# An unbroken warm-up, a reordered front and another load order in a fused attention and feed-forward kernel

## The chip, the cores and the metric

The kernel runs on one core of a Trainium2 chip. The metric is device time in microseconds (us) of one execution, lower is better. Most executions of the kernel before agree within 0.3%. A run is called slow when it is over 1.5% above the fastest of the same kernel; comparisons use the other runs ("fast" ones). One run of each kernel was also profiled; all places in time below are from those profiles, counted from the first instruction.

## The reference, cut to what matters

```python
# x (8, 8, 512, 64), state (8, 8, 32, 64); w_in (512, 2048), w_out (2048, 512)
a  = softmax(scale * x @ state^T);   xread = a @ state      # per batch and head
a2 = softmax(scale * state @ x^T);   sread = a2 @ x
y  = concat(xread, sread) over the sequence, heads side by side   # (8 * 544, 512)
h  = y @ w_in;  r = max(h, 0);  g = s * r * r + b;  out = g @ w_out
```

The kernel never forms xread: it multiplies state with a 512-column part of w_in first (M), and then h = a @ M.

## The kernel before

The work is eight batches. A batch needs x with its two inner axes exchanged (xT), the state likewise (stT), the scores T = state @ x^T, E = exp(T), the sums D, the four products M with a cast each, then 16 times h, relu, square, and products with w_out (o). Each step is handed to a small planner with an estimate of its duration. The planner simulates the engines and fixes, before anything runs, the order in which every engine executes its steps. At run time an engine takes its instructions in that order, also when one waits for a load and others behind it are ready: in the profile of the changed kernel, below, VectorE stands 4.08 us before a cast whose load is late, with a copy ready behind it, and TensorE 3.30 us.

The parts that the change and the argument touch (cuts marked):

```python
# 1. The loads. GpSimd issues the large ones in this order; "stf1" is the state of the
#    second and third batches, issued by SyncE behind a memset that GpSimd makes.
SEQ = "wi0 x1 wi1 stf1 wo0 wi2 wo1 wi3 wo2 wo3 x2 sb x3 x4 x5"
...
elif it[0] == "stf1":       # -3.0: the planner expects it 3.0 us before the load ahead of it
    load(key, 0.3, -3.0, late(stf1, st_v[:, NG : NB_HW * NG, :]), [it], after=3.4)

# 2. The casts of the state: one step of VectorE serves the second and third batches
add(DV(0.4), 0, lambda e: cast_st(e, stf1, NG, n1), [("stf1",)], [("st", 1), ("st", 2)])

# 3. The state of the other five: GpSimd makes a 128x2 copy first, only so that the load
#    isn't issued before the last w_out part has landed
def load_stf2(e):
    nc.gpsimd.tensor_copy(stf2[:, 0, 0:2], wo[3][:, 0, 0:2])
    nc.sync.dma_start(stf2, st_v[:, NB_HW * NG :, :])

# 4. xT of the first three batches (NB_HW = 3) is made by TensorE (xT_mm) and copied by
#    VectorE; of the others by four DMA transposes each, issued by SyncE
...
# 5. Warm-up: the planner puts a product of a zero tile wherever TensorE has nothing ready
def filler(e):
    mm(ob[1], warm[:, 0:P], warm)
for step in sorted(plan.order(filler, 14.0, landed), key=lambda t: t[:2]):
    step[3](step[2])
```

The softmax here doesn't subtract the row's maximum and nothing guards it: scores larger than these inputs give would overflow.

Of the kernel before, what the change touches and what calls it, by code (L numbers as in the profile page):

```python
# [13 lines left out]
class Plan:  # L14
# [13 lines left out]
    def order(self, filler, fill_until, ready):  # L28
# [24 lines left out]
        free_at["PE"] = 1.2  # L53
        mode, channel, log, now, done_n = False, 7.0, [], 0.0, 0
        times = []

        def soon(i):
# [14 lines left out]
        while done_n < len(ops):  # L72
            for e in free_at:
# [29 lines left out]
                if best is None:  # L103
                    fill = 0.43 if now < 7.0 else 0.22
                    if e == "PE" and now < fill_until and not any(since[i] < now + fill for i in cand[e]):
                        free_at[e] = now + fill
                        times.append(free_at[e])
                        log.append((now, len(log), "PE", filler, "warm", free_at[e]))
                    continue
# [47 lines left out]
def kernel(  # L157
# [119 lines left out]
    def late_dma(dst, src):  # L277
# [5 lines left out]
    K = dict(  # L283
        h1=4.4, hs=0.6, M0=-5.6, M1=0.9, T1=0.0, x2=24.6, T2=23.7, D2=27.2, M2=35.3, V0=27.7, V1=21.3, u=12.3,
        us=5.1, pd1=12.5, o0=13.1, o2=23.0, w=26.2, r=0.5, T=-9.8, D=3.1, Mb=6.4, V=8.6, S=3.6, S0=0.1, E=-0.5,
        L=-6.2, a4=-4.7, Mc=1.5, pd=13.4, solo=2.0, hsr=-4.1, Ssr=0.0,
    )
# [61 lines left out]
    for i in range(4):  # L349
        add(  # L350
            (DV(0.35), AC(0.5)),
            -29 + i,
            cast_x0(i),
            [("xf", i)],
            [("x", 0, i)],
            [("u", f"xf{i // 2}"), ("xn", "x0")],
        )
# [44 lines left out]
    nc.gpsimd.tensor_copy(gate, ident16[:, 0:2])  # L402
    SEQ = "wi0 x1 wi1 stf1 wo0 wi2 wo1 wi3 wo2 wo3 x2 sb x3 x4 x5"
    seq = [(t,) if t in ("stf1", "sb") else (t[:-1], int(t[-1])) for t in SEQ.split()]
    for n, it in enumerate(seq):
        key = -40 + n
        if it[0] == "wi":
            load(key, 0.8, 4.2 if it[1] == 0 else 2.8, load_wi(it[1]), [it], after=3.4)
        elif it[0] == "wo":
            load(key, 0.8, 2.8, load_wo(it[1]), [it], after=3.4)  # L410
        elif it[0] == "x":
            b = it[1]
            load(
                key, 0.9, 2.9 if b == 1 else 3.9, load_x(b),
                [("x", b, i) for i in range(4)], [("xn", f"x{b}")], after=3.4,
            )
        elif it[0] == "stf1":
            load(key, 0.3, -3.0, late(stf1, st_v[:, NG : NB_HW * NG, :]), [it], after=3.4)
        else:
            load(key, 0.15, 0.1, late(s_bc, moe_s.to_broadcast((P, 1))), [("s",)], after=3.4)  # L420
            load(key + 0.1, 0.15, 0.1, late(b_bc, moe_b.to_broadcast((P, 1))), [("b",)], after=3.4)
# [28 lines left out]
    add(("SP", 1.5), 18, dma_stT, [("st", 3)], [("stT", b) for b in range(NB_HW, B)], land=("tp", 3.0))  # L450

    def xT_of(b, h):
        if b < NB_HW:
            return A[b]["xT"][:, h % 2, h // 2]
        return A[b]["xT"][:, h]

    def dma_xT(b, i):
        def fn(e):
            if "xT" not in A[b]:
                A[b]["xT"] = apool.tile([P, H, 2, P], FP16, name=f"xT_{b}", tag="xT")  # L460
                A[b]["stT"] = stTd[:, (b - NB_HW) * NG : (b - NB_HW + 1) * NG]
            nc.sync.dma_start_transpose(
                A[b]["xT"][:, 2 * i : 2 * i + 2].rearrange("p h k q -> p (h k) q"),
                xn[b][:, 2 * i : 2 * i + 2].rearrange("p h c d -> p (h c d)"),
            )

        return fn
# [34 lines left out]

    def xT_copy(b, i):
        def fn(e):
            if i == 0:
                A[b]["xT"] = apool.tile([P, 2, 4, 2, P], FP16, name=f"xT_{b}", tag="xT")
            copy_on(e, A[b]["xT"][:, i], A[b][f"xTps{i}"])

        return fn

    def st_T(b, g, q, m):
        h = head_of(g, q)
        return A[b]["stT"][64 * m : 64 * m + 64, h // 4, 32 * (h % 4) : 32 * (h % 4) + 32]

# [146 lines left out]

    for b in range(B):
        if b < 2:
            kT = kD = kx = -10 if b == 0 else K["T1"]
            kM = [8 * c + (K["M0"] if b == 0 else K["M1"]) for c in range(4)]
        elif b == 2:
# [8 lines left out]
        if b < NB_HW:  # L675
# [3 lines left out]
            add(DV(0.2), kx, stT_copy(b), [("stps", b)], [("stT", b)], [stps] + stT_b)  # L679
            for i in range(2):  # L680
                ps = ("att", f"xTps{b}{i}")
                xs = [("x", b, 2 * i), ("x", b, 2 * i + 1)]
                add(PEt(0.45), kx + 0.1 * i, xT_mm(b, i), xs, [("xTps", b, i)], [ps, xn_b, xT_b])
                add(
                    (DV(0.62), AC(1.1)) if b == 9 else DV(0.62), kx + 0.1 * i, xT_copy(b, i),
                    [("xTps", b, i)] + ([("xT", b, 0)] if i else []), [("xT", b, i)], [ps, xT_b],
                )
        else:
            stT_b = []
            for i in range(4):  # L690
                add(
                    ("SP", 1.2), kx + 0.1 * i, dma_xT(b, i),
                    [("x", b, i)], [("xT4", b, i)], [xT_b, xn_b], ("tp", 3.0),
                )
        xT_need = [("xT", b, 0), ("xT", b, 1)] if b < NB_HW else [("xT4", b, i) for i in range(4)]
        E_b = [("E0", f"E{b}0"), ("E1", f"E{b}1"), ("rs", f"rs{b}")]
        Tb = [("att", f"T{b}0"), ("att", f"T{b}1")]
        if b == 0:
            for g in range(2):
                add(  # L700
                    PEt(0.2), kT, T_mm(b, [g]), [("stT", b), xT_need[g]] + ([("T", b, 0)] if g else []),
                    [("T", b, g)], Tb + [xT_b] + stT_b + E_b, tiled=True,
# [6 lines left out]
        for g in range(2):  # L709
# [3 lines left out]
            add(  # L713
                AC(0.73), kT + K["E"] + g, E_exp(b, g), [("T", b, g)] + ([("E", b, 0)] if g else []),
                [("E", b, g)], Tb + [Eb, rs],
            )
            add(PEt(0.22), kD, D_mm(b, g), [("E", b, g)], [("D", b, g)], [Eb, Dps, Rb, a4b])
            add(AC(0.53), kD + K["L"] + g, D_ln(b, g), [("D", b, g)], [("Dl", b, g)], [Dps])
            add(AC(0.53), kD + K["L"] + g, D_exp(b, g), [("Dl", b, g)], [("R", b, g)], [Dps, Rb])
            add(DV(0.34), kD + K["a4"], a4_mul(b, g), [("R", b, g)], [("a4", b, g)], [Eb, Rb, a4b])  # L720
# [10 lines left out]
        for c in range(4):  # L731
# [5 lines left out]
            for g in range(2):  # L737
                kc = kM[c] + K["Mc"]
                add(
                    (AC(0.53), DV(0.6)) if g else (DV(0.6), AC(0.53)), kc, M_cast(b, c, g),  # L740
                    [("Mps", b, c)], [("M", b, c, g)], [mp[g], M_b],
                )
# [77 lines left out]
    for b in range(B):  # L820
        for f in range(NKF):
# [7 lines left out]
            )  # L829
            add((AC(0.5), DV(0.6)) if b < 2 else AC(0.5), k + K["r"], relu(b, f, S), [("h", b, f)], [("r", b, f)], [hb, gb])  # L830
            add(DV(0.335), k, square(b, f), [("r", b, f)], [("g", b, f)], [gb])
# [256 lines left out]
    def filler(e):  # L1088
        mm(ob[1], warm[:, 0:P], warm)

    landed = {
        "ident": 3.2, "stf": 4.8, ("xf", 0): 3.8, ("xf", 1): 4.7, ("xf", 2): 5.8, ("xf", 3): 6.8,
    }
# [30 lines left out]
```

## Time and profile before

| | before |
|---|---|
| time, median of 4 runs | 216.97 us (216.32 to 216.99) |
| span of the profiled run | 215.0 us |
| TensorE busy | 204.7 us, 95% |
| matrix work of its own at full clock, worked out below | 193.3 us |
| TensorE's last product | 208.4 us |

I took the start of every product from the trace and gave each kind the time that it takes in an unbroken row at full clock: 0.2155 us for 512 columns, 0.0555 for a transpose, 0.0428 for a product of M, 0.0223 for one of T, 0.0109 for one of V. What half and full clock are is read from the profile of before: 512-column products in a row start 0.427 us apart up to 9.94 us and 0.216 apart from 10.97 on, and the trace's record of the granted clock opens at 10.56, with 1.00; later in a profile half clock is a granted clock of 0.50. Elapsed time minus the own work begun so far is the **time lost so far**: fillers, holes and half clock together. A reading at one moment says how far a kernel is behind; the difference between two moments says where it fell behind. Before has lost 13.8 us at 25 us, and 15.1 at the end: all but 1.4 us of the loss lies in the first 25 us.

### The profile page before, as it was taken

To read this page: it belongs to the slowest core of one execution; us is meant where nothing else is said; L and a number is where in the kernel's file an instruction comes from. 1 tells how busy PE (TensorE), PEld (TensorE's weight loads), DVE (VectorE), ACT (ScalarE), POOL (GpSimd) and SP (SyncE) were. 2 spreads that over 40 slices of the span, in tenths; PEclk is the share of its full clock that TensorE was granted. 3 is DMA by queue.
4 is the path that set the end of the run, shared out by engine and by line. 5 is a ranking of instruction groups with operands and counts; after the bars stand their busy time and mean duration, and the time that the engine had idled before them with its cause. 6 is when DMAs were issued, how large, how long until landed. Compare 5 with 4: busy or idle time off the path is not lost.

```text
span 215.0 us, 4963 instructions
## 1 busy us (share of the span) xinstructions
PE 204.7 (95%) x1976; PEld 132.6 (62%) x1976; DVE 176.0 (82%) x412; ACT 132.5 (62%) x288; POOL 37.3 (17%) x60
## 2 busy tenths in 40 slices
PE   5998999999999999999999999999999999999980
PEld 1452334544567676667666766676667777888860
DVE  1258999999998969999999998999999988776750
ACT  4478997695385965795579558855786544532000
POOL 4923100050134261012101210121012102100000
PEclk9999999999999999999999999999999999999997
DMA  6999999999379996453164203311232011210221
GB/s 191 188 196 184 207 204 196 184 153 213 88 128 189 148 200 127 100 102 102 49 100 109 99 30 45 82 52 66 59 81 85 17 48 55 101 36 15 99 83 64
DMA packets 41415, 24.05 MB, mean 112 GB/s; under 512 B 25776, under 2 KB 39600, under 8 KB 41392
## 3 DMA queue, kind: packets, MB, share of 16 engines
q0 software_dynamic: 13840, 15.21, 35.9%
q1 hardware_dynamic: 26992, 8.40, 23.6%
q8 instruction: 15, 0.25, 0.5%
q10 hardware_dynamic: 560, 0.13, 0.3%
q14 instruction: 8, 0.07, 0.1%
HBM read 17.37 MB, written 8.91 MB: 122 GB/s over the span
## 4 chain that ended last, share of the span: by engine, by line
PE 84%; ACT 5%; DVE 5%; DMA 2%; issue 1%; SPq 0%
PE o L209 47%; PE h L209 22%; PE Mps L209 4%; PE h_sr L209 3%; PE osr L209 3%; ACT g L773 2%; DMA xf<-in_x_dram 2%; DVE g L779 1%; PE D L209 1%; ACT M L310 1%; PE V L209 1%; PE xTps L209 1%; PE T L209 1%; ACT E L540 1%; DVE u L858 1%
## 5 line engine op out<-in xcount | busy, mean ns | idle before, releaser
L773 ACT ACTIVATE g<-h 128x512 f16<-128x512 f32 x126 | 73.4, 601 | 41.5 <-PE h L209 41.3
L209 PE MATMUL h<-a,M 128*128 128x512 f16 x256 | 73.8, 380 | 0.6 <-ACT g L773 0.5
L779 DVE TENSOR_TENSOR g<-g 128x512 f16<-128x512 f16 x128 | 52.7, 420 | 3.9 <-ACT g L773 2.3
L209 PEld LDWEIGHTS <-pd 128*128 128x128 f16 x448 | 42.6, 98 | 20.0 <-issue 3.4
L209 PEld LDWEIGHTS <-g 128*128 128x128 f16 x400 | 39.0, 98 | 19.6 <-issue 0.6
L209 PE MATMUL o<-u,pd 128*128 128x256 f16 x336 | 45.9, 273 | 0.0
L209 PE MATMUL o<-wo,g 128*128 128x256 f16 (+1 forms) x288 | 45.5, 297 | 0.1
L1030 POOL DMA_DIRECT2D out_dram<-c x24 | 16.3, 679 | 103.8 <-DVE c L1018 101.0
L209 PEld LDWEIGHTS <-M 128*128 128x128 f16 x256 | 24.1, 98 | 13.2 <-issue 4.6
L310 ACT CAST M<-Mps 128x512 f16<-128x512 f32 x45 | 25.3, 595 | 7.1 <-PE Mps L209 7.1
L1018 DVE SCALAR_TENSOR_TENSOR c<-o,s_bc,bias_bc 128x512 f32<-128x512 f32 x28 | 21.0, 750 | 7.4 <-PE o L209 6.5
L795 DVE TENSOR_TENSOR pd<-g 128x1024 f16<-128x1024 f16 x28 | 19.2, 686 | 0.3
L1018 DVE SCALAR_TENSOR_TENSOR c<-o,s_bc,c 128x512 f32<-128x512 f32 x21 | 15.7, 750 | 1.8 <-PE o L209 1.6
L209 PE MATMUL o<-wo,pd 128*128 128x256 f16 x112 | 16.2, 273 | 0.0
L209 PE MATMUL o<-u,g 128*128 128x256 f16 x112 | 15.5, 273 | 0.0
L312 DVE CAST M<-Mps 128x512 f16<-128x512 f32 x19 | 13.0, 687 | 2.0 <-PE Mps L209 1.9
L773 ACT ACTIVATE g_sr<-h_sr 128x256 f16<-128x256 f32 x16 | 6.1, 383 | 10.5 <-PE h_sr L209 10.4
L540 ACT ACTIVATE E<-T 128x256 f16<-128x256 f32 x32 | 11.8, 389 | 1.1 <-PE T L209 1.1
L806 DVE TENSOR_TENSOR pd<-g,pd 128x512 f16<-128x512 f16 x28 | 11.8, 422 | 0.4
L387 POOL DMA_DIRECT2D xn<-in_x_dram x13 | 10.4, 818 | 8.6 <-DMA wi<-in_moe_w_in_dram 4.0
L804 DVE TENSOR_TENSOR pd<-g,pd 128x512 f16<-128x512 f16 x28 | 11.7, 418 | 0.0
L559 ACT ACTIVATE D<-D 128x512 f32<-128x512 f32 x16 | 9.6, 601 | 2.0 <-PE D L209 1.9
(71 smaller groups left out, 165.1 us busy)
## 6 DMA issues: line engine op xcount, KB each, us to landing
out_dram<-c POOLq DMA_DIRECT2D x24, 256.0 KB, 2.5
xn<-in_x_dram POOLq DMA_DIRECT2D x5, 512.0 KB, 22.4
wi<-in_moe_w_in_dram POOLq DMA_DIRECT2D x4, 512.0 KB, 13.2
wo<-in_moe_w_out_dram POOLq DMA_DIRECT2D x4, 512.0 KB, 18.8
xf<-in_x_dram SPq DMA_DIRECT2D x4, 256.0 KB, 3.4
out_dram<-osb POOLq DMA_DIRECT2D x4, 256.0 KB, 4.1
xn<-in_x_dram POOLq DMA_DIRECT2D x8, 128.0 KB, 4.4
out_dram<-c SPq DMA_DIRECT2D x4, 256.0 KB, 2.5
```

The costliest lines, as they stand in the source:

```text
L209: return nc.tensor.matmul(out, lhsT, rhs, start=start, stop=stop, tile_position=tp, is_transpose=is_transpose, skip_group_check=True,)
L310: nc.scalar.copy(dst, src)
L312: ENG[e].tensor_copy(dst, src)
L387: nc.gpsimd.dma_start(out=xn[b][:, h0:h1].rearrange("p h c d -> p h (c d)"), in_=x[b, h0:h1].rearrange("h (q c) d -> q h (c d)", q=P),)
L540: nc.scalar.activation(a["E"][g][:, 256 * m : 256 * m + 256], a["T"][m][:, g, :], AF.Exp, scale=scale, accum_out=a["rs"][:, g, m : m + 1],)
L773: nc.scalar.activation(g_of(name, f), OSB["h", name, f], AF.Relu)
L779: ENG[e].tensor_mul(g_of(name, f), g_of(name, f), g_of(name, f))
L795: nc.vector.tensor_tensor(pd[:, :, 0:2], g4[:, :, 1:2, :].to_broadcast((P, 2, 2, t)), g4[:, :, 0:4:3, :], ALU.subtract,)
L804: nc.vector.tensor_tensor(pd[:, :, 2], g4[:, :, 3], pd[:, :, 0], ALU.subtract)
L806: nc.vector.tensor_tensor(pd[:, :, 3], g4[:, :, 2], pd[:, :, 2], ALU.subtract)
L1018: nc.vector.scalar_tensor_tensor(t, src, s_bc, add, ALU.mult, ALU.add)
L1030: ENG[e].dma_start(dst[:, rows:SCH:2, hD * h : hD * h + hD], SN[b, name])
```

## The change

The intent: bring the array to full clock sooner (nine fillers in a row), let the second batch's attention start before w_in is there (its x is loaded first), take the third batch's 16 transposes off TensorE, and give the planner more places to set (new keys, ScalarE or VectorE for every relu). Cut to its core:

```diff
+        for k in range(9):                       # planner: nine fillers in one row at 1.2 us
+            log.append((free_at["PE"], len(log), "PE", filler, "warm", free_at["PE"] + 0.43))
+            free_at["PE"] += 0.43
...
-                    fill = 0.43 if now < 7.0 else 0.22
+                    fill = 0.22
...
-    SEQ = "wi0 x1 wi1 stf1 wo0 wi2 wo1 wi3 wo2 wo3 x2 sb x3 x4 x5"
+    SEQ = "x1 wi0 stf1 wo0 wi1 wi2 wi3 wo1 wo2 wo3 sb x2 x3 x4 x5"
...
-            load(key, 0.3, -3.0, late(stf1, st_v[:, NG : NB_HW * NG, :]), [it], after=3.4)
+            load(key, 0.3, -2.2, late(stf1, st_v[:, NG : NB_HW * NG, :]), [it], after=3.4)
...
+    NB_T = 2                                     # xT by TensorE for two batches, not three
-        if b < NB_HW:
+        if b < NB_T:
             return A[b]["xT"][:, h % 2, h // 2]
...                                               # K: most keys changed, some 20 added;
                                                  # half copies of xT for the first batch
```

More of the change, by code (lines that the diff above doesn't have):

```diff
@@ L53, in order @@
         free_at["PE"] = 1.2
-        mode, channel, log, now, done_n = False, 7.0, [], 0.0, 0
+        mode, channel, log, now, done_n = False, 7.2, [], 0.0, 0
         times = []
+        for k in range(9):
+            log.append((free_at["PE"], len(log), "PE", filler, "warm", free_at["PE"] + 0.43))
+            free_at["PE"] += 0.43
         def soon(i):
@@ L283 @@
     K = dict(
-        h1=4.4, hs=0.6, M0=-5.6, M1=0.9, T1=0.0, x2=24.6, T2=23.7, D2=27.2, M2=35.3, V0=27.7, V1=21.3, u=12.3,
-        us=5.1, pd1=12.5, o0=13.1, o2=23.0, w=26.2, r=0.5, T=-9.8, D=3.1, Mb=6.4, V=8.6, S=3.6, S0=0.1, E=-0.5,
-        L=-6.2, a4=-4.7, Mc=1.5, pd=13.4, solo=2.0, hsr=-4.1, Ssr=0.0,
+        h1=4.3, hs=0.6, M0=0.0, M1=0.9, T1=-1.4, x2=24.6, T2=25.1, D2=23.6, M2=34.0, V0=27.7, V1=29.1, u=11.8,
+        us=2.5, pd1=11.8, o0=12.8, o2=20.7, w=24.9, r=0.5, T=-9.7, D=3.1, Mb=6.4, V=0.6, S=3.6, S0=0.4, E=-0.7,
+        L=-4.9, E0=-7.0, L0=-5.0, E1=-7.0, L1=0.5, a4=-7.1, Mc=1.5, pd=13.4, solo=2.0, f0=0.0, f1=8.0, mc=0.3,
+        hsr=-2.4, Ssr=4.1, jE00=0.0, jE01=-1.8, jL00=-1.9, jL01=-0.3, jR00=0.0, jR01=0.0, jE10=2.5, jE11=0.0,
+        jL10=0.0, jL11=0.0, jR10=0.0, jR11=1.8, jM0=0.0, jM1=0.0,
     )
@@ L350 @@
         add(
-            (DV(0.35), AC(0.5)),
+            AC(0.5) if i < 3 else (DV(0.35), AC(0.5)),
             -29 + i,
@@ L407 @@
         if it[0] == "wi":
-            load(key, 0.8, 4.2 if it[1] == 0 else 2.8, load_wi(it[1]), [it], after=3.4)
+            load(key, 0.8, 2.62, load_wi(it[1]), [it], after=3.4)
         elif it[0] == "wo":
-            load(key, 0.8, 2.8, load_wo(it[1]), [it], after=3.4)
+            load(key, 0.8, 2.62, load_wo(it[1]), [it], after=3.4)
         elif it[0] == "x":
@@ L413 @@
             load(
-                key, 0.9, 2.9 if b == 1 else 3.9, load_x(b),
+                key, 0.9, {1: 3.4, 2: 2.9}.get(b, 3.9), load_x(b),
                 [("x", b, i) for i in range(4)], [("xn", f"x{b}")], after=3.4,
@@ L460, in fn @@
                 A[b]["xT"] = apool.tile([P, H, 2, P], FP16, name=f"xT_{b}", tag="xT")
-                A[b]["stT"] = stTd[:, (b - NB_HW) * NG : (b - NB_HW + 1) * NG]
             nc.sync.dma_start_transpose(
@@ L501, in xT_mm, with xT_copy @@
         return fn
-    def xT_copy(b, i):
+    def xT_copy(b, i, q0=0, q1=4):
         def fn(e):
-            if i == 0:
+            if "xT" not in A[b]:
                 A[b]["xT"] = apool.tile([P, 2, 4, 2, P], FP16, name=f"xT_{b}", tag="xT")
-            copy_on(e, A[b]["xT"][:, i], A[b][f"xTps{i}"])
+            copy_on(e, A[b]["xT"][:, i, q0:q1], A[b][f"xTps{i}"][:, q0:q1])
         return fn
@@ L512, in st_T @@
         h = head_of(g, q)
-        return A[b]["stT"][64 * m : 64 * m + 64, h // 4, 32 * (h % 4) : 32 * (h % 4) + 32]
+        t = A[b]["stT"] if b < NB_HW else stTd[:, (b - NB_HW) * NG : (b - NB_HW + 1) * NG]
+        return t[64 * m : 64 * m + 64, h // 4, 32 * (h % 4) : 32 * (h % 4) + 32]
     def T_mm(b, gs):
@@ L662 @@
     for b in range(B):
+        kE, kL = K["E"], K["L"]
         if b < 2:
             kT = kD = kx = -10 if b == 0 else K["T1"]
+            kE, kL = (K["E0"], K["L0"]) if b == 0 else (K["E1"], K["L1"])
             kM = [8 * c + (K["M0"] if b == 0 else K["M1"]) for c in range(4)]
@@ L679 @@
             add(DV(0.2), kx, stT_copy(b), [("stps", b)], [("stT", b)], [stps] + stT_b)
-            for i in range(2):
+            for i in range(2 if b < NB_T else 0):
                 ps = ("att", f"xTps{b}{i}")
@@ L683 @@
                 add(PEt(0.45), kx + 0.1 * i, xT_mm(b, i), xs, [("xTps", b, i)], [ps, xn_b, xT_b])
-                add(
-                    (DV(0.62), AC(1.1)) if b == 9 else DV(0.62), kx + 0.1 * i, xT_copy(b, i),
-                    [("xTps", b, i)] + ([("xT", b, 0)] if i else []), [("xT", b, i)], [ps, xT_b],
-                )
+                if b == 0:
+                    for n in range(2):
+                        add(
+                            DV(0.35) if i == 0 else (DV(0.35), AC(0.56)), -29.5 + 10 * i, xT_copy(b, i, 2 * n, 2 * n + 2),
+                            [("xTps", b, i)] + ([("xTh", b, 0, 0), ("xTh", b, 0, 1)] if i else []),
+                            [("xTh", b, i, n)], [ps, xT_b],
+                        )
+                else:
+                    add(
+                        DV(0.62), kx + 0.1 * i, xT_copy(b, i),
+                        [("xTps", b, i)] + ([("xT", b, 0)] if i else []), [("xT", b, i)], [ps, xT_b],
+                    )
         else:
             stT_b = []
+        if b >= NB_T:
             for i in range(4):
@@ L694 @@
                 )
-        xT_need = [("xT", b, 0), ("xT", b, 1)] if b < NB_HW else [("xT4", b, i) for i in range(4)]
+        xT_need = [("xT", b, 0), ("xT", b, 1)] if b < NB_T else [("xT4", b, i) for i in range(4)]
         E_b = [("E0", f"E{b}0"), ("E1", f"E{b}1"), ("rs", f"rs{b}")]
@@ L700 @@
                 add(
-                    PEt(0.2), kT, T_mm(b, [g]), [("stT", b), xT_need[g]] + ([("T", b, 0)] if g else []),
+                    PEt(0.2), kT, T_mm(b, [g]), [("stT", b), ("xTh", b, g, 0), ("xTh", b, g, 1)] + ([("T", b, 0)] if g else []),
                     [("T", b, g)], Tb + [xT_b] + stT_b + E_b, tiled=True,
@@ L713 @@
             add(
-                AC(0.73), kT + K["E"] + g, E_exp(b, g), [("T", b, g)] + ([("E", b, 0)] if g else []),
+                AC(0.73), kT + kE + g + K.get(f"jE{b}{g}", 0.0), E_exp(b, g), [("T", b, g)] + ([("E", b, 0)] if g else []),
                 [("E", b, g)], Tb + [Eb, rs],
@@ L717 @@
             add(PEt(0.22), kD, D_mm(b, g), [("E", b, g)], [("D", b, g)], [Eb, Dps, Rb, a4b])
-            add(AC(0.53), kD + K["L"] + g, D_ln(b, g), [("D", b, g)], [("Dl", b, g)], [Dps])
-            add(AC(0.53), kD + K["L"] + g, D_exp(b, g), [("Dl", b, g)], [("R", b, g)], [Dps, Rb])
+            add(AC(0.53), kD + kL + g + K.get(f"jL{b}{g}", 0.0), D_ln(b, g), [("D", b, g)], [("Dl", b, g)], [Dps])
+            add(AC(0.53), kD + kL + g + K.get(f"jR{b}{g}", 0.0), D_exp(b, g), [("Dl", b, g)], [("R", b, g)], [Dps, Rb])
             add(DV(0.34), kD + K["a4"], a4_mul(b, g), [("R", b, g)], [("a4", b, g)], [Eb, Rb, a4b])
@@ L737 @@
             for g in range(2):
-                kc = kM[c] + K["Mc"]
+                kc = kM[c] + K["Mc"] + K.get(f"jM{b}", 0.0)
                 add(
                     (AC(0.53), DV(0.6)) if g else (DV(0.6), AC(0.53)), kc, M_cast(b, c, g),
-                    [("Mps", b, c)], [("M", b, c, g)], [mp[g], M_b],
+                    [("Mps", b, c)], [("M", b, c, g)], [mp[g], M_b], spare=K["mc"],
                 )
@@ L829 @@
             )
-            add((AC(0.5), DV(0.6)) if b < 2 else AC(0.5), k + K["r"], relu(b, f, S), [("h", b, f)], [("r", b, f)], [hb, gb])
+            add((AC(0.5), DV(0.6)), k + K["r"], relu(b, f, S), [("h", b, f)], [("r", b, f)], [hb, gb], spare=K["f0"] if b < 2 else K["f1"])
             add(DV(0.335), k, square(b, f), [("r", b, f)], [("g", b, f)], [gb])
@@ L1091 @@
     landed = {
-        "ident": 3.2, "stf": 4.8, ("xf", 0): 3.8, ("xf", 1): 4.7, ("xf", 2): 5.8, ("xf", 3): 6.8,
+        "ident": 3.2, "stf": 4.8, ("xf", 0): 3.9, ("xf", 1): 4.75, ("xf", 2): 6.2, ("xf", 3): 6.4,
     }
```

## The prediction

> **What bounds the kernel now.** I read the page's busy shares first, then the busy table by stretch, then TensorE's instructions in order of time, then the chain of work that ended last, and at the end the landing times of the loads.
>
> ```profile
> PE 204.7 (95%) x1976; PEld 132.6 (62%) x1976; DVE 176.0 (82%) x412; ACT 132.5 (62%) x288; POOL 37.3 (17%) x60
> PE 84%; ACT 5%; DVE 5%; DMA 2%; issue 1%; SPq 0%
> 0.00:10.00 10.00, 7.47 (x38) 3.27 (x38) 2.40 (x8) 4.50 (x9) 6.85 (x14) 1.00 0.89 191
> 20.00:30.00 10.00, 9.53 (x61) 3.43 (x60) 8.94 (x25) 9.72 (x20) 0.94 (x2) 1.00 1.24 203
> 50.00:60.00 10.00, 10.00 (x142) 4.98 (x140) 9.55 (x23) 4.92 (x10) 0.54 (x1) 1.00 0.73 104
> 150.00:170.00 20.00, 20.00 (x216) 13.77 (x201) 18.12 (x42) 14.60 (x32) 2.03 (x3) 1.00 0.26 69
> ```
>
> The columns of the last four lines are the stretch in us, its length, busy us of PE, PEld, DVE, ACT and POOL (instruction counts in brackets), the granted clock, the DMA share and GB/s. From 50 us on TensorE is full, without a hole, until its last instruction. So the kernel is a fixed amount of matrix work plus whatever TensorE does not spend on that work in the first 50 us. A change gains only by taking away matrix work, or by taking away filler and holes in that first part. Everything after 50 us shifts along with it.
>
> The busy share hides the filler: products of a zero tile ("o<-warm") count as busy. TensorE's own list shows them, and what they stand between:
>
> ```profile
> 1.19 2.31 PE L209 MATMUL o<-warm 128*128 128x512 f16 x5 [1.19 <-DVE warm L224]
> 4.64 0.61 PE L209 MATMUL xTps<-ident,xn 128*128 128x128 f16 x4 [1.14 <-ACT xn L310]
> ...
> 8.66 1.06 PE L209 MATMUL o<-warm 128*128 128x512 f16 x2
> 9.51 0.64 PE L209 MATMUL D<-E,bones 128*128 128x512 f16 x1
> ...
> 12.48 0.41 PE L209 MATMUL Mps<-wi,stT 64*32 64x512 f16 x8
> 12.82 1.69 PE L209 MATMUL o<-warm 128*128 128x512 f16 x7
> 14.35 1.03 PE L209 MATMUL h<-a,M 128*128 128x512 f16 x4
> ...
> 17.97 0.90 PE L209 MATMUL Mps<-wi,stT 64*32 64x512 f16 x8
> 19.56 0.74 PE L209 MATMUL D<-E,bones 128*128 128x512 f16 x2 [0.69 <-ACT E L540]
> 20.14 1.09 PE L209 MATMUL h<-a,M 128*128 128x512 f16 x4
> 21.15 0.41 PE L209 MATMUL Mps<-wi,stT 64*32 64x512 f16 x8
> 21.50 1.90 PE L209 MATMUL o<-wo,g 128*128 128x512 f16 x8
> ...
> 38.19 1.06 PE L209 MATMUL xTps<-ident,xn 128*128 128x128 f16 x16
> ```
>
> Lengths overlap in this list, so I use differences of starts. There are 24 fillers before 14.35 us. Of these 14.35 us only about 2.1 are the kernel's own work at full speed; the rest is filler, half speed and waiting. After that the largest hole is the group at 17.97: the next one starts 1.59 us later, where eight such products otherwise take 0.34 (12.48 to 12.82), so 1.25 us are lost. Between 24.75 and 27.34 two groups of four h products take 1.31 and 1.28 us where four take 0.86, some 0.85 us more.
>
> The chain of waits says who holds TensorE there: from 16.84 to 26.06 us it runs over ScalarE alone (relu, casts of M, the exponentials of the second batch), which is busy 9.72 of 10 us.
>
> [...] the fillers at 8.66 start 0.425 apart, the seven at 12.82 take 1.53 us, 0.219 each, and the switch lies at about 10.4 us. The granted clock in the table above stays at 1.00 through this, so it doesn't show it. The 1.14 us hole before 4.64 is the break which the change closes.
>
> [...] The trace shows them landing in the order of issue. By issue time plus time to landing: first w_in part 3.4 + 6.6 = 10.0; second batch's x 4.3 + 9.3 = 13.6; second w_in part 5.2 + 11.1 = 16.3; first w_out part 6.2 + 12.7 = 18.9; third w_in part 6.9 + 15.2 = 22.1. So 2.6 us for each weight part, 3.6 for an x, about 3.2 with the state load between. [...]
>
> [...] Here SyncE issues them, 1.19 to 1.93 us for each xT piece, median 3.6 us to landing, 8.9 for the transposes of a that are issued while loads still run.
>
> **The change part by part.** The order of the changed kernel's instructions is known from building it; its times are not.
>
> 1. Third batch's x is transposed by DMA instead of TensorE. It takes away 16 products, 38.19 to 39.08, 0.89 us of TensorE on the path, and two VectorE copies (1.28 us, off the path, since VectorE leads no wait there). It adds four transposes to SyncE, and moves that batch's scores to well after the first output products of the second batch. Gain 0.89.
>
> 2. The fillers: nine in one row after 1.2 us (eleven before the first real product), 25 in all against 24. I expect the array warm at 5 to 8 us instead of 10.4. That makes the first batch's transposes, T and D shorter (0.83 us for eight transposes at 7.83, 0.44 for eight at 15.21; D 0.43 to 0.22), and the filler in front of a ready instruction too. About 1 us off the chain to the first h. I count it as zero by itself, since part 3 makes that first h wait for a load.
>
> 3. Second batch's x in front, first w_in part behind. By the landings above, x comes at 10.0 + 1.0 = 11.0 and w_in at 13.6, where x came. The M products then start at about 13.8, take 0.34, and the cast (0.6 to 0.69) with two hand-overs of about 0.1 makes the first h start at about 15.0: 0.65 later than 14.35. But in place of fillers the second batch's 16 transposes (0.88), state transpose (0.12), T (0.36) and M (0.34) now stand ahead of it or at it. Then D of both batches and four h follow, and the next M products need the second w_in part, which is fourth in the queue: about 18.9. At 18.9 + 0.2 the M products of both batches run, 0.34 + 0.23, and at 19.67 this much is done: all transposes, T, D and two M of both batches, four h. The old kernel has done that and two h more at 21.50, so it was there at 21.50 - 0.87 = 20.63. Gain 0.96.
>
> 4. The first batch's steps: four half copies of xT (a 1024-column copy takes 0.69, a 256-column one 0.28, so a half about 0.42), one of them on ScalarE, the first three casts of x on ScalarE as they were. T can start some 0.3 us earlier, again hidden behind the load. The choice of engine for relu in later batches is hardly used: VectorE does one relu instead of two and 17 casts of M instead of 19. Zero.
>
> 5. From 20 to 50 us the same ScalarE work has to pass; the holes there (0.45 and 0.42 at 24.75 and 26.06, 0.31 at 33.2) I leave as they are. The old hole at 17.97 is part of the sum in 3.
>
> 6. Cost: later w_out parts. The second moves from 7.65 + 17.0 = 24.7 to 27.2, and the third batch's DMA transposes: stTd is issued at 44.60 and takes 3.01, so three of the four xT pieces come after 47.6, end issuing at 47.6 + 3 x 1.45 = 52.0 and land about 3 later, near 55, just about where T of the third batch stands in the new order; the fourth batch's follow at once. I put half a chance on a hole of 0.2, the rest being absorbed. Cost 0.1.
>
> Sum: 0.89 + 0.96 - 0.1 = 1.75 us off 216.99, or 215.2. Spread over the runs of before is 0.67 us. I round to 215.1, because the earlier full clock may also shorten the way to the first h a little, of which I counted nothing.
>
> **The rivals.**
> A: the warm-up is what counts. Then the first h would come about a microsecond before 14.35, and with the 0.89 and the reordering the time would fall by 2.5 to 3, to about 214.2. For it: TensorE is at half speed for two thirds of the way to the first h. Against it: TensorE's products there are few, and w_in cannot be in before about 13.6.
> B: ScalarE takes all of the gain of the start back, since it is 97% busy from 20 to 30 us and the chain lies on it. Moving the second batch's exponentials forward into ScalarE's holes (1.39 us before its logarithm at 10.19, 0.70 and 0.78 at 14.98 and 16.84) speaks against it. It would leave only 0.89: 216.1.
> C: the DMA transposes of the third batch come late and TensorE stands still at T or the D after it, for 1 to 3 us. For it: the arithmetic of part 6, and 8.9 us to landing while loads run. Against it: the loads are over by 47.6 and the order leaves output products in front of T. It would give 216 to 218.
> D: later w_out parts stop VectorE, which takes its work strictly in order, at the sums over w_out; squares stand behind them. 0.5 us at most: 215.6.
>
> **Range and chances.** The parts that I trust are 0.89 (removed work on a full engine) and about 1 for the start; A adds up to 1, B, C or D take up to 1 or a little more. 8 times in 10: 214.0 to 216.5. Two per cent is 4.3 us, as much as all the holes that I found after 14.35 and the transposes together, so faster by over 2% is 0.03. Slower by over 2% needs C at its worst: 0.02. Within 2%: 0.95.
>
> **What would show it.** Part 1: 32 xT transposes instead of 48 in TensorE's list. Part 2: spacing of 0.22 from 5 to 8 us on. Part 3: first h at 14.7 to 15.3, led by the w_in load; second w_in part landing near 18.9; the first o product about 1 us earlier than the old one after taking off the h done by then. Part 6: no hole over 0.3 us before T of the third and fourth batch. TensorE's end 1.7 to 1.9 before 208.7. I am wrong if the first h comes before 14.35 (A), if the lead is 1 us at 20 and gone at 30 (B), or if TensorE waits on a transpose near 55 us (C).

## The result, and the profile after

| | before | changed |
|---|---|---|
| median | 216.97 us | 220.50 us |
| range, runs | 216.32 to 216.99, 4 | 219.26 to 220.66, 4 |
| span of the profiled run | 215.0 us | 218.8 us |
| mean granted clock, profiled run | 0.993 | 0.981 |

The changed kernel is slower: ratio 1.0158, 95% interval 1.0116 to 1.0199. (Ratios here are the mean time of one kernel's fast runs over that of the other's in the same rounds, so not quite the ratio of the medians.) The time lies outside the predicted range, on the other side of zero; that it stays within 2% of before, to which the prediction gave 0.95, is right.

The page's busy shares and its chain of waits, changed kernel:

```profile
PE 205.1 (94%) x1961; PEld 131.9 (60%) x1961; DVE 170.6 (78%) x408; ACT 134.4 (61%) x292; POOL 38.8 (18%) x60
PE 79%; DVE 9%; DMA 6%; ACT 2%; POOL 1%; issue 1%
PE o L212 44%; PE h L212 21%; DMA stf<-in_state_dram 5%; DVE g L797 4%; PE Mps L212 3%; PE h_sr L212 3%; PE osr L212 3%; PE D L212 1%; PE T L212 1%; PE V L212 1%; DMA ident<-ident_const 1%; DVE u L878 1%; DVE pd L813 1%; ACT R L573 1%; DVE a L619 1%
```

TensorE's busy time is as before, which misleads: there are 15 products fewer. What is new is one load in the chain, stf (the state), 5% of the span, a load to which the prediction gave no landing time. The start of that chain in order of time (start, length, what):

```profile
5.52 10.34 DMA stf<-in_state_dram
...
15.88 0.88 DVE st L317 x2
...
16.81 0.40 PE stTps L212 x2
```

The second batch's state takes 10.34 us from issue to landing. VectorE's cast of it and TensorE's transpose follow at once. TensorE and VectorE around it, in order of time (in brackets the idle time before, and its releaser):

```profile
12.22 1.07 PE L212 MATMUL xTps<-ident,xn 128*128 128x128 f16 x16 [0.83 <-DMA xn<-in_x_dram]
13.12 0.38 PE L212 MATMUL o<-warm 128*128 128x512 f16 x1
16.81 0.40 PE L212 MATMUL stTps<-ident,st 128*128 128x128 f16 x2 [3.30 <-DVE st L317]
...
19.72 1.89 PE L212 MATMUL h<-a,M 128*128 128x512 f16 x4
```

```profile
15.88 0.86 DVE L317 CAST st<-stf 128x256 f16<-128x256 f32 x2 [4.08 <-DMA stf<-in_state_dram]
16.67 0.67 DVE L317 COPY xT<-xTps 128x1024 f16<-128x1024 f16 x1
```

VectorE stands 4.08 us before the cast, although the 16 transposes whose result it is to copy next have been there since 13.1. TensorE stands 3.30 us: the planner has put the second batch's state transpose ahead of the first batch's M and h. So the first h comes at 19.72, not at 15.0. Why the planner put it there can be worked out from its code, where a load's landing is an estimate: x 7.2 + 3.4 = 10.6 us, the first w_in part 10.6 + 2.62 = 13.22, and the state 13.22 - 2.2 = 11.02. It landed at 15.86, 4.8 us later. In the kernel before, the planner expected it at 13.9, and the cast, later in the order, waits for nothing at 14.40:

```profile
14.40 0.69 DVE L312 CAST st<-stf 128x256 f16<-128x256 f32 x2
```

The standstill costs twice. The busy table of the changed kernel, cut every 3.41 us, so that the changes of the trace's clock record (15.93 and 22.76) are edges (columns as in the prediction: the last three are granted clock, DMA share, GB/s):

```profile
12.52:15.93 3.41, 0.98 (x15) 0.65 (x12) 0.04 (x1) 0.12 (x1) 1.02 (x4) 1.00 1.24 203
15.93:19.34 3.41, 2.14 (x34) 0.87 (x34) 3.14 (x7) 0.59 (x1) 1.60 (x2) 0.50 1.33 204
19.34:22.76 3.42, 3.42 (x19) 1.12 (x9) 2.31 (x4) 2.71 (x11) 0.87 (x1) 0.50 1.24 207
22.76:26.20 3.44, 2.98 (x26) 1.06 (x25) 2.50 (x8) 3.41 (x7) 0.88 (x1) 1.00 1.24 205
```

After the stretch of 3.41 us in which TensorE worked 0.98, the granted clock is 0.50 for 6.83 us. Four h products that took 1.68 us from 19.72 on (to the next start at 21.40) took 0.86 in the kernel before.

The time lost so far, read as explained above. Its last row is at 208 us; "own" is the sum of own work:

```text
at us   before  changed
 15      12.01   12.33
 25      13.77   18.12
 50      12.90   17.03
 75      13.41   17.53
100      13.71   17.95
208      15.14   19.37
own     193.29  192.40
```

(Both sink by about 1 us between 25 and 50, where my times for a few kinds of product are too dear; only differences within a row count.) At 25 us the changed kernel is 4.35 us behind. After that it loses 1.25 us and before 1.37: in sum nothing more happens. With 0.89 us less of own work this gives the 3.4 us by which TensorE's last product is later (211.82 against 208.39). So the whole difference of this pair arises in the first 25 us.

### The profile page after: what moved, and what is told of

Its sections match the earlier page's. It is cut to its first block, busy times and chain, and to the rows that moved or that the text cites.

```text
span 218.8 us, 4964 instructions
## 1 busy us (share of the span) xinstructions
PE 205.1 (94%) x1961; PEld 131.9 (60%) x1961; DVE 170.6 (78%) x408; ACT 134.4 (61%) x292; POOL 38.8 (18%) x60
## 4 chain that ended last, share of the span: by engine, by line
PE 79%; DVE 9%; DMA 6%; ACT 2%; POOL 1%; issue 1%
PE o L212 44%; PE h L212 21%; DMA stf<-in_state_dram 5%; DVE g L797 4%; PE Mps L212 3%; PE h_sr L212 3%; PE osr L212 3%; PE D L212 1%; PE T L212 1%; PE V L212 1%; DMA ident<-ident_const 1%; DVE u L878 1%; DVE pd L813 1%; ACT R L573 1%; DVE a L619 1%
## 5 line engine op out<-in xcount | busy, mean ns | idle before, releaser
L212 PEld LDWEIGHTS <-pd 128*128 128x128 f16 x448 | 43.3, 98 | 18.8 <-issue 2.0
L315 ACT CAST M<-Mps 128x512 f16<-128x512 f32 x47 | 26.8, 600 | 15.7 <-PE Mps L212 15.7
L212 PE MATMUL o<-u,g 128*128 128x256 f16 x112 | 16.0, 273 | 0.0
L317 DVE CAST M<-Mps 128x512 f16<-128x512 f32 x17 | 11.5, 683 | 0.8 <-PE Mps L212 0.8
L392 POOL DMA_DIRECT2D xn<-in_x_dram x13 | 10.6, 854 | 7.5 <-DMA wi<-in_moe_w_in_dram 5.7
```

The lines of the kernel that those rows point to most:

```text
L212: return nc.tensor.matmul(out, lhsT, rhs, start=start, stop=stop, tile_position=tp, is_transpose=is_transpose, skip_group_check=True,)
L315: nc.scalar.copy(dst, src)
L317: ENG[e].tensor_copy(dst, src)
L392: nc.gpsimd.dma_start(out=xn[b][:, h0:h1].rearrange("p h c d -> p h (c d)"), in_=x[b, h0:h1].rearrange("h (q c) d -> q h (c d)", q=P),)
```

## The experiments

All gave correct results. The first question is whether the late state is the cause. Most edits freeze the planner's order and change one thing in it, in front of the last loop (`at(name)` is the place of the step that makes `name`). The medians of before in the same rounds lie between 216.55 and 217.19 us throughout; ratios are to those.

### Keeping the clock through the wait

```diff
# changed kernel, order frozen
+i = at(("stps", 1))                              # second batch's state transpose
+steps[i:i] = [(0, 0, "PE", filler, "warm", 0)] * 16
```

> The changed kernel with sixteen more products of the zero tile in front of the second batch's state transpose, where TensorE stood idle from 13.5 to 16.8 us; nothing else moved. My theory: the loss has two parts, a wait for the second and third batch's state (landed at 15.86 us) and, because of the idle time, half clock from about 16 to 22.6 us. Then here the granted clock stays at 1.00 from 10 to 30 us, the first h stays at 19.0 to 19.8 us, and the time falls by 1.5 to 2.5 us, to 218 to 219. Rival 1 (the wait is all of it, half clock lies beside ScalarE and VectorE work anyway): under 0.5 us gained. Rival 2 (the DMA transposes of the third batch cost it): nothing gained.

220.01 us, ratio 1.0147 (1.0111 to 1.0184). In the profile no stretch is at half clock before the end (mean granted clock 0.996 against 0.981); the first h comes at 18.99 instead of 19.72, and at 25 us the time lost is 16.61 instead of 18.12. Of these 1.51 us, 0.48 were there before the first product after the wait: the state's transpose starts at 16.33 instead of 16.81, because VectorE's two casts took 0.49 us instead of 0.86, for a reason that no run here tested. The other 1.03 are what half clock cost by 25 us. Yet the time hardly falls, and my 218 to 219 missed (under 0.5 us by the medians, as rival 1 had it, and the intervals of the ratios overlap); from 35 to 75 us this kernel is 1.1 to 1.9 us ahead of the changed one, and ends 0.8 ahead. Part of the gain is given back where TensorE waits for the third batch's xT (0.51 us ahead of 59.66, in the middle of T): a first sign of a second obstacle. Its profile shows another new thing, taken up below: GpSimd's tiny copy took 5.34 us (0.23 in the changed kernel).

### Loading the state at the start

```diff
# changed kernel
     for i in range(4):
         nc.sync.dma_start(xf_part(i), xf_heads(x0_v, i))
+    nc.sync.dma_start(stf1, st_v[:, NG : NB_HW * NG, :])
...
-            load(key, 0.3, -2.2, late(stf1, st_v[:, NG : NB_HW * NG, :]), [it], after=3.4)
+            load(key, 0.3, -2.2, lambda e: None, [it], after=3.4)
```

> The changed kernel with the state of the second and third batch loaded at the very start, right behind the first batch's x; every instruction but this load in the same place. My theory: the cast of that state no longer stops VectorE; the first h comes at about 16.7 us, led by the first w_in part (15.4 us + M + cast), TensorE's idle time stays under 2.5 us and the clock at 1.00; time falls by 3 to 4.5 us, to 216 to 217.5. Rival (the late first w_in part holds everything up by itself): the first h stays near 19 us and under 1 us is gained.

218.70 us, ratio 1.0108 (1.0050 to 1.0166). The front is mended: TensorE waits for no state, the first h comes at 15.54, and the time lost at 25 us is 13.12, 5.0 less than in the changed kernel and 0.65 less than in before. The end shows only a part of it, and my 216 to 217.5 missed, because of this place in TensorE's list:

```profile
60.25 0.42 PE L212 MATMUL T<-xT,stTd 64*32 64x256 f16 x12
63.47 0.28 PE L212 MATMUL T<-xT,stTd 64*32 64x256 f16 x2 [2.80 <-DMA xT<-xn]
```

That is the T of the fourth batch, standing for a DMA transpose of its x. The time lost goes from 12.13 at 60 us to 15.37 at 75. In the changed kernel the same T came later and found its xT there. This is a hidden second wall.

### The first w_in part ahead of x again

```diff
# changed kernel, order frozen
+i, j = at(("x", 1, 0)), at(("wi", 0))
+steps[i], steps[j] = steps[j], steps[i]
```

> The changed kernel with the first w_in part again ahead of the second batch's x in the queue; every engine's order is otherwise that of the changed kernel. My theory: the state still lands at about 15.5 us and VectorE and TensorE stand behind it in order, so little is gained, 0 to 0.7 us (TensorE waits for x till 13.6 and may idle less before the state comes). Rival (the order of these two loads is what cost the time): 2 us or more gained, first h near 16.

219.48 us, ratio 1.0120 (1.0087 to 1.0154). My expectation of the state's landing missed: with w_in in front it was there early enough for the cast to start at 13.03 us. So this run doesn't separate load order from late state as I meant it to; by the medians it gained 1.0 us, between my 0 to 0.7 and the rival's 2. The first h came at 16.70; T of the fourth batch again waited, 1.90 us ahead of 63.59.

### Both

The two edits together.

> Both edits: early state and the first w_in part ahead of the second batch's x. My theory: now the second batch's x (about 13.6) is what its transposes wait for, in front of M and h in TensorE's order; the first h near 15.5 us; time 215 to 216.5, not slower than with the early state alone. Rival (with the state early, x first is right): 0.5 to 1.5 us slower than with the early state alone.

218.02 us, ratio 1.0045 (1.0012 to 1.0079; one slow run of 220.92 left out). First h at 15.99, time lost at 25 us 13.68, and this time T of the third batch waits, 1.03 us ahead of 57.19. My 215 to 216.5 missed; that it is faster than with the state alone isn't shown, since the two intervals overlap.

### All four transposes of the third batch in front

The wall looked like a matter of order in SyncE's queue. SyncE's issues before, then in the changed kernel (start, length in the queue, what, how many):

```profile
44.60 3.01 SPq L446 DMA_TRANSPOSE stTd<-st  x1
47.72 5.81 SPq L462 DMA_TRANSPOSE xT<-xn  x4
```

```profile
47.95 1.33 SPq L451 DMA_TRANSPOSE stTd<-st  x1
49.33 10.56 SPq L468 DMA_TRANSPOSE xT<-xn  x7
```

Seven in a row instead of four; the fourth batch's are the last of them, and end 6.4 us later (59.9 against 53.5). With the state loaded at the start:

```diff
# the kernel with the state at the start, order frozen
+moved = [steps.pop(at(("xT4", 2, i))) for i in (1, 2, 3)]
+i = at(("xT4", 2, 0)) + 1
+steps[i:i] = moved
```

> The changed kernel with the early state, and in SyncE's queue all four transposes of the third batch's x together, right where the first of them stood, ahead of the transposes of a and of stTd; nothing else moved. My theory: with the state early, the wall is SyncE's queue, where seven xT transposes stand behind stTd (48 to 59 us) and TensorE waited 2.80 us at T of the fourth batch; here T of the third and fourth batch find their data, no hole over 0.3 us after 50 us, TensorE ends near 207.2 and the time is 215.0 to 216.0, faster than before by 0.5 to 1%. Rival (transposes issued under the loads are slow, 8.9 us to landing, and push the transposes of a and stTd back by as much): the hole moves to V or to T of the fourth batch and the time stays over 217.5.

220.54 us (217.54 to 222.44, two slow runs left out of the ratio), ratio 1.0118 (1.0065 to 1.0171). My expectation missed, the rival's held: in the profile the wall only moved. (One of the six runs took 217.54 us, so the loss isn't the same in every run.)

```profile
36.03 9.09 SPq L469 DMA_TRANSPOSE xT<-xn  x4
45.21 5.21 SPq L629 DMA_TRANSPOSE aT<-a  x4
```

Issued from 36.03 on, the four took 9.09 us (5.81 in before, from 47.72 on), and the transposes of a for the first two batches now stand behind them:

```profile
52.17 0.30 PE L212 MATMUL V<-xn,aT 128*32 128x64 f16 x16 [0.80 <-DMA aT<-a]
54.17 0.30 PE L212 MATMUL V<-xn,aT 128*32 128x64 f16 x16 [1.70 <-DMA aT<-a]
```

The time lost rises from 12.63 at 50 us to 17.24 at 60, part of it from another 3.41 us at half clock.

The same regrouping on the changed kernel, with its late state:

> The changed kernel with only SyncE's queue regrouped as in the run with the early state, and the late state left as it is. In the changed kernel TensorE is so late at T of the third batch that it doesn't wait there; so by my theory nothing is gained, 219.5 to 220.7 us. Rival (the transposes of the third batch are what costs the changed kernel its time): 218 or less.

219.81 us, ratio 1.0136 (1.0116 to 1.0156). First h at 19.57, half clock from 16.36 to 23.19, time lost at 25 us 18.12 exactly as in the changed kernel. Behind such a front the order in SyncE's queue matters little.

### Third batch by DMA, alone

Part 1 of the prediction by itself, on the kernel before.

```diff
# kernel before; the planner makes its order anew: the third batch's T comes at 60.65 us
# (41.99 in the kernel before, 60.78 in the changed one)
+    NB_T = 2                                     # used in place of NB_HW for xT alone
```

> The kernel before with nothing but the third batch's x transposed by DMA instead of TensorE (the planner then puts T of that batch later by itself). Part 1 of my prediction says 0.89 us faster, 216.1 to 216.4. My theory now: four more transposes, 1.2 to 2.3 us each in SyncE's queue while the loads run, push T, V or the fourth batch's T back, so TensorE shows new holes between 48 and 68 us and the 0.89 is lost or more: 217 to 219.

222.54 us, ratio 1.0271 (1.0246 to 1.0295): the slowest of all, from the part that I had counted on most. Its front is fine (13.34 us lost at 25). SyncE's queue now runs late by some 8 us (two transposes of a that were issued from 58.67 on are issued from 67.21), and it shows at a V product:

```profile
74.47 0.79 PE L209 MATMUL V<-xn,aT 128*32 128x64 f16 x32 [3.05 <-DMA aT<-a]
```

The time lost goes from 13.1 at 70 us to 19.7 at 90: 3.05 us of waiting, some more holes, and half clock from 72.98 to 79.81. GpSimd's copy took 0.34 us here, so a long copy isn't needed for this wall.

### State at the start, third batch by TensorE again

```diff
# the kernel with the state at the start; the planner makes its order anew
-    NB_T = 2
+    NB_T = 3
```

> The changed kernel with the state of the second and third batch loaded at the start, and the third batch's x transposed by TensorE again. SyncE's queue then has as many transposes before 60 us as the kernel before. My theory: both walls are gone; first h at 15.3 to 15.8 us, no hole at T of the fourth batch nor at V, time 215.5 to 217.0, level with before or up to 0.7% faster. Rival (a third cause is left in the new order): 218 or more.

217.41 us, ratio 1.0025 (1.0008 to 1.0041), a little above the 215.5 to 217.0 that I expected. It has the 16 transposes on TensorE again and is still 1.3 us faster than with DMA (0.8% by the ratios; these are of different rounds). So two steps bring the changed kernel back to before, nearly: 220.5, then 218.7 with the state early, then 217.4 with the third batch on TensorE. What is left of the change brings no gain: 0.25% slower than before. The planner made its order anew here, so more than the transposes moved. In this profile the second w_in part came at 20.1 us, 1.2 later than in the profile with the third batch by DMA, and the lead at 25 us is gone (14.02); V waits 1.41 us for aT ahead of 62.23.

### Warm-up alone, load order alone

```diff
# kernel before, order frozen: nine fillers in a row
+i = at(("xTps", 0, 0))
+steps[i:i] = [(0, 0, "PE", filler, "warm", 0)] * 4
# and, as another kernel: x1 and wi0 exchanged, as in the experiment above
```

> The kernel before with nothing but four more zero products after its first five, so that nine stand in one row in front of the first transposes. By rival A of my prediction the unbroken warm-up is worth about a microsecond at the first h: spacing 0.22 from 5 to 8 us on, first h at 13.4 to 13.8 instead of 14.35, time 216.0 to 216.5. By my own account of part 2 the chain gets shorter, but what comes out at the end is between 0 and 0.8 us; a gain under 0.2 us would say that the work after it (ScalarE from 17 to 26 us) takes it back.

216.47 us, ratio 0.9977 (0.9956 to 0.9998). The trace's clock record opens, with 1.00, at 5.63 us instead of 10.56, and the first h comes at 13.04 instead of 14.35. Of this 1.3 us, 0.5 remain: the second batch's transposes then wait 0.54 us for x.

> The kernel before with nothing but the swap of the first two loads: second batch's x ahead of the first w_in part. My theory: the first M products wait for w_in, 13.2 to 15.4 us instead of 10.0, the first h comes at 14.9 to 16.5 instead of 14.35, and since the order behind it is unchanged nothing is won by the earlier x: 0.5 to 1.5 us slower than before. Rival (the chain to the first h is bound by the first batch's own steps, so w_in has slack): within 0.3 us of before.

219.73 us, ratio 1.0105 (1.0065 to 1.0144; one slow run of 223.43 left out). The exchange alone costs, by the medians 2.5 us and so more than the 0.5 to 1.5 that I expected: first h at 15.53, time lost at 25 us 15.10 against 13.77. In the old order of steps there is nothing to do with an early x.

### What worked, put together

Nine fillers in a row and the state loaded at the start, everything else as before.

> The kernel before with the nine unbroken zero products (as in the run with them alone) and, besides, the state of the second and third batch loaded at the start. In the run with the zero products alone TensorE lost 0.7 us at the second batch's transposes, whose x landed at 14.6. My theory: that x now lands near 12.5 to 13.2, this hole goes, the time falls to 215.6 to 216.3, 0.2 to 0.4 us under the zero products alone. Rival (ScalarE from 17 to 26 us takes it back): the same as with the zero products alone, 216.2 to 216.7.

215.64 us (215.21 to 216.07), ratio 0.9936 (0.9919 to 0.9953). It beats both kernels.

```profile
1.19 3.62 PE L209 MATMUL o<-warm 128*128 128x512 f16 x9 [1.19 <-DVE warm L224]
...
13.02 1.03 PE L209 MATMUL h<-a,M 128*128 128x512 f16 x4
13.88 0.61 PE L209 MATMUL xTps<-ident,xn 128*128 128x128 f16 x8
```

With the state out of the row of loads, the second batch's x lands at 13.75 (later than the 12.5 to 13.2 expected, but in time for 13.88), and the wait of the warm-up kernel at this place is gone. 12.91 us are lost at 25, and no wall follows.

### The late cast, and GpSimd's copy

If the load cannot come early, the order can wait for it: VectorE casts the state after the first batch's casts of M, TensorE takes the second batch's state transpose, T, D and M after the first two h.

```diff
# changed kernel, order frozen; after(a, names) moves the steps that make names behind a
+after(("M", 0, 0, 1), [("st", 1)])
+after(("r", 0, 1), [("stps", 1), ("stT", 1), ("T", 1, 0), ("E", 1, 0), ("E", 1, 1), ...,
+                    ("Mps", 1, 0), ("M", 1, 0, 0), ("M", 1, 0, 1)])
```

> The changed kernel with every load as it is, the state landing late too; only the order of instructions differs: VectorE casts the second batch's state after the first batch's cast of M instead of ahead of the second batch's xT copies, and TensorE takes the second batch's state transpose, T, D and first M after the first two h instead of ahead of them. My theory: the late state only hurts because it stands in front of the first batch's work in two strictly ordered queues; here the first h waits for w_in alone (15.4 + M + cast) and comes at 16.5 to 17 us instead of 19.72, TensorE idles under 3 us, and the time falls by 1 to 2 us (part of it may be taken back by the transposes of the third and fourth batch): 218.5 to 219.5. Rival (the late landing itself, not the place in the order, sets the pace): the first h comes earlier, but the time stays within 0.5 us of the changed kernel.

220.53 us (one slow run of 224.24 left out of the ratio), ratio 1.0195 (1.0160 to 1.0229). The first h came at 15.53, 4.2 us earlier, and at 25 us 1.94 us less were lost than in the changed kernel, but the time did not fall: my expectation missed. (Its profiled run is the slow one and serves here only for where the waits are.) T of the fourth batch waited 2.95 us for xT; the mean granted clock of the run was 0.977. SyncE issued the load of the other batches' state at 38.00, against 33.68 in the changed kernel, since GpSimd's copy ahead of it took 5.08 us. (With the state at the start it took 3.32 us, and the load was issued at 35.05.) Such a copy, in before and in the kernel with the 16 fillers:

```profile
32.36 0.35 POOL L424 CAST stf<-wo 128x2 f32<-128x2 f16 x1 [9.12 <-DMA wo<-in_moe_w_out_dram]
```

```profile
33.13 5.34 POOL L429 CAST stf<-wo 128x2 f32<-128x2 f16 x1 [9.07 <-DMA wo<-in_moe_w_out_dram]
```

In the second kernel VectorE runs nothing but operations on two operands in SBUF, back to back, from before 33.13 until a cast out of PSUM starts at 38.35, and GpSimd's copy ends at 38.47. Two more profiles show the same: with the state at the start the copy took 3.32 us and ended at 35.02, and the cast started at 34.90; with SyncE's queue regrouped besides, 2.99 us, 35.45 and 35.32. But in before, in the changed kernel, with the third batch by DMA alone and in the kernel put together from what worked, the copy took 0.35, 0.23, 0.34 and 0.44 us beside VectorE operations of the same kind; so what makes it long isn't shown. To test whether it matters for the time, ScalarE makes the copy:

```diff
-        nc.gpsimd.tensor_copy(stf2[:, 0, 0:2], wo[3][:, 0, 0:2])
+        nc.scalar.copy(stf2[:, 0, 0:2], wo[3][:, 0, 0:2])
```

> The late-cast order of e12_late, with one more edit: the 128x2 copy that releases the load of the third to eighth batches' state is made by ScalarE and not by GpSimd. Theory A (in e12_late GpSimd's copy was held for 5.08 us beside VectorE's products of two operands in SBUF, and so the state load, which stands ahead of all the transposes in SyncE's queue, was late): the load issues near 33 us and not at 38.0, the fourth batch's state transpose lands 1 to 2.5 us earlier, the 2.9 us hole ahead of the fourth batch's T shrinks or goes, and the time is 218.5 to 219.5. Rival (the number of transposes in SyncE's queue is what is late, whatever the load does): the load issues earlier, but the hole stays above 2 us and the time is within 0.5 us of e12_late, 220.0 to 221.0.

221.15 us (219.79 to 221.72), ratio 1.0209 (1.0188 to 1.0229). This one is inconclusive. ScalarE reached its 0.18 us copy only at 36.79, and SyncE issued the load at 37.00, not near 33. The hole at the fourth batch's T is gone, but not for the expected reason: this run's front had lost 17.69 us by 25 (10.24 us at half clock, 14.69 to 24.93), and T came late enough for its data.

```profile
11.28:14.69 3.41, 1.57 (x26) 0.94 (x23) 2.70 (x5) 1.78 (x4) 1.13 (x4) 1.00 1.23 201
14.69:18.10 3.41, 2.59 (x22) 0.99 (x22) 1.43 (x5) 0.60 (x1) 0.94 (x2) 0.50 1.33 203
```

How much of the wall is due to the long copy therefore stays open. That the additional transposes suffice for one is shown by the kernel with the third batch by DMA alone.

## Why the prediction was wrong, point by point

The time lost at 25 us splits the result. Adding the readings: before to the kernel with the state at the start, 13.77 to 13.12; from there to the one with the late state and fillers, 16.61; from there to the changed kernel, 18.12 (split as in the first experiment). Each reading is of one profile. Kernels that are alike up to 25 us read 18.12 and 18.12 (changed, and with SyncE's queue regrouped), 13.12 and 13.34 (state at the start, without and with the regrouping), but 16.18 and 17.69 (late cast, copy by GpSimd or by ScalarE), where only the second fell to half clock (10.24 us of it from 14.69 on); so terms of some tenths are no more than indications.

| term | predicted | measured |
|---|---|---|
| own work taken off TensorE | -0.89 | -0.89 |
| the new front, once its state is there | -0.96 | -0.65 |
| waiting for the second batch's state | not in the sum | +3.49 |
| VectorE's slower cast of the state | not in the sum | +0.48 |
| half clock after that wait | not in the sum | +1.03 |
| 25 us to 208 us | +0.1 | -0.12 |
| sum | -1.75 | +3.34 |

The last 0.1 to TensorE's 3.43 lies after 208 us.

**Part 3 is the step that failed.** It wrote that "the second batch's 16 transposes (0.88), state transpose (0.12), T (0.36) and M (0.34) now stand ahead of it or at it", and looked up landings for x and both w_in parts only. For the state it gave no landing; it appears solely as delay in the row ("about 3.2 with the state load between"). In the order that was known, a transpose of the state and VectorE's cast stood ahead of the first h, and the load landed at 15.86. The sum's first h at 15.0 is what the planner had too (14.96, when its code is run without the chip), with its state at 11.02. In the five profiles that have the changed kernel's loads in this order the state landed between 14.48 and 16.03, so an estimate taken from one trace needs a margin as well. That the rest of the arithmetic was sound is seen where the state is early: x landed at 10.79 (predicted 11.0), M at 13.36 (13.8), first h at 15.54 (15.0), M of both batches done at 19.94 (19.67).

**Half clock after a hole was left out altogether.** The prediction counted half clock for the start only. What it cost shows at 25 us (1.03); in the time of the whole kernel it isn't shown (220.01 us with the fillers against 220.50, intervals overlapping). In the changed kernel the fastest run, 219.26 us, had the highest mean clock, 0.987 against 0.975 to 0.981; that a lower clock goes with a longer run isn't so everywhere (third batch by DMA alone: 222.38 us at 0.975, 223.85 at 0.985).

**Part 1: the work came off, the gain did not.** "Gain 0.89" holds for TensorE's own work. By itself, in the order that the planner then makes, the move costs 2.7%.

**Part 6 and rival C were right in kind and off in size.** The cost of late transposes was put at 0.1. In the changed kernel no such hole shows, which looks like a confirmation and is none: the front is so late that the data is there. With the front mended the hole is 2.80 us. My own figures held it: issuing ends at 52.0 for the third batch, four more at 1.45 each give 57.8, and with 3 to landing 60.8. The fourth batch's T came at 60.25 when the front was good. I stopped the sum at the third batch, and charged issue times from the old queue: seven took 1.63 each (11.43 us) in the kernel with the state at the start. Rival C's 1 to 3 us at T was the right size, at the next batch.

**Part 2** was right: fillers are 0.22 apart from 6.34 us on in the changed kernel, and its clock record opens at 5.69; the 5 to 8 us given for full clock were my estimate. **Rival A** was true of the old order alone: first h at 13.04, ahead of 14.35, but 0.23% in time, not 1%. **Part 5**, the later part left as it is, held for the changed kernel. **Part 4** and **rivals B and D** were not tested singly. The gain wasn't taken back by a full ScalarE: the chain from 5.52 to 15.86 us is the state load, and ScalarE was busy for 0.12 us of the 3.41 from 12.52 on.

## What to carry to other kernels

When an engine's order is fixed in advance, list for every instruction that moves ahead of the critical one all of its inputs, small loads included, and put a landing time beside each: 128 KB to which nobody gave one cost about 3.5 us at the front here. If a planner makes the order, compare the landings that it assumes with a trace (11.02 assumed, 15.86 measured). After a repair read the trace again from the repaired place on, since a late front hides the next wall. Work moved from a full engine into a queue is only a gain if that queue's last element, added up to the end, is still in time.
